# Moving the pair sums of the second key chunk to GpSimd and reordering the front units of the maxima in an attention block

## The chip, the cores and the metric

The kernel runs on one core of a Trainium2 chip, as one launch. The metric is the device time of that launch in microseconds (us). A core has five engines that each work through their own queue in order: TensorE (PE in the profile; PEld are its weight loads), VectorE (DVE), ScalarE (ACT), GpSimd (POOL) and SyncE (SP, which here issues nearly all DMAs). They wait for each other by semaphores. The stated times are 1812.58, 1813.54 and 1829.46 us; their median is 1813.54.

## The reference

One transformer block with adaptive layer norm, sequence 2048, width 512, 32 heads of 16, inner width 1792, all in float32:

```
mod = silu(c) @ w_mod                    # sa, ca, ga, sb, cb, gb
h = layernorm(x) * (1 + ca) + sa
q, k, v = h @ wqkv                       # 32 heads of width 16
o = softmax(q k^T / 4) v                 # full, 2048 x 2048 per head
x = x + ga * (o @ wo)
h = layernorm(x) * (1 + cb) + sb
out = x + gb * (gelu(h @ w1 + b1) @ w2 + b2)
```

## The kernel before, in words

Every matmul operand is split into a rounded high part and a low part, and a product is made of three matmuls (`mm3`, line 290): high by high, low by high, high by low.

**Units.** The heads are taken in 8 groups of 4, the queries in 4 blocks of 512. A unit `u` is one group and one block of queries; group `u // 4` gives its keys. For each unit the kernel first needs the largest score of every query and head, and then, in a second pass, the exponentials and their product with the values. The maxima of the first nine units (0 to 8, `NU1 = 9`) are made early, between the matmuls of the projections. Those of the other units are made within the attention, nine units ahead of the exponentials.

**Pair maxima.** The early maxima use a trick that halves the reductions: the maximum of a and b is (a + b)/2 + |a - b|/2. For groups 0 to 3 (key chunks `k` = 0 and 1) the kernel therefore stores, besides the keys, sums and differences of the keys of two neighbouring blocks of 512 (`kpm_d`). They are made in `proj_qk`: for an even block `b` the key projection is copied from PSUM to `k2` (line 308); for the odd block VectorE makes sum and difference from PSUM and `k2` (line 313), ScalarE rounds them to the high part (line 314), GpSimd makes the low part (line 320), and two DMAs store them (line 322). Each result is read by a front unit as `kpm[u // 4]`, loaded by `build_k` (line 350). In `pair_slot` a slot "V" multiplies queries by the differences (line 417) and ScalarE takes the absolute value (line 424); a slot "U", two places later, multiplies by the sums, and VectorE's custom instruction adds and reduces (line 428). Each slot has two matmuls of 48 rows that use different rows of the array. When the last slot of a unit is done, `max_rows` finishes its maxima with two small GpSimd operations, a transpose on VectorE (line 445), and four small stores (line 448).

**The stage.** After a first loop over the four blocks come 34 items in a fixed order. Items 0 to 9 are the last ten tiles of the values (tiles 6 to 15 of 16; `proj_v`, line 333 copies a tile from PSUM to one of the `vst` buffers, line 335 stores it). Items 10 to 17 are the projections with chunk k = 1, items 18 to 25 with k = 2, items 26 to 33 with k = 3; within a chunk the blocks b = 0 to 3 follow each other, keys (w = 1) ahead of queries (w = 0). Between the matmuls of an item stand "visits": from item 6 on five visits of two slots each, six in items 7, 14, 21 and 28. Unit number v in the order begins with visit 16 v and needs 16 slots of each kind; 144 visits fill the stage exactly. PSUM has two banks (`sc`) for the projections here and six (`mx`) for the slots. A projection's evacuation is line 303 on ScalarE (high part), line 304 on VectorE (low part), and what is left of it (`rest`: stores and GpSimd work) is issued with the first visit of the next item. Functions that a unit leaves over (`todo`) are run one at the end of each item.

**Loads.** At item 12 the keys of group 0 for the attention are loaded into `kq[0]`, then the values of group 0 (`load_v(0)`), then the weights of chunk 3. At item 21 the pair sums of group 2 go into the tile `kts[0]`, which units 0 to 3 have used; unit 8 needs them. At item 32 the keys of group 2 go into `kts[1]`, which units 4 to 7 have used; unit 9, the first maximum inside the attention, needs them. After the stage the keys of group 1 go into `kts[0]`.

**The weights of a chunk** are split in `split_w`: ScalarE rounds (line 172), GpSimd subtracts (line 174), at item 12 for chunk 2 and at item 20 for chunk 3.

Of the kernel before, what the change touches and what calls it, by code (L numbers as in the profile page):

```python
# [31 lines left out]
KR = 3 * DH  # L32
KX = KR + 2
NM = 32
NU1 = 9
FILL0 = 6
VISIT = 2
OP0 = 1
# [12 lines left out]
def block_kernel(ctx: ExitStack, tc: tile.TileContext, x, wqkv, wo, w1, b1, w2, b2, c, w_mod, out):  # L51
# [59 lines left out]
    b2_b = const.tile([P, D], F32, name="b2_b")  # L111
    b1_c = const.tile([P, NF], F32, name="b1_c")

    lcm, lend = pool("lend")
# [7 lines left out]
    wslots = [wpool.tile([P, KC, D], FR, name=f"w{i}") for i in range(2)]  # L122
    vwcm, vwpool = pool("vwpool", side="right")
    vslots = [vwpool.tile([P, KC, D], FR, name=f"wv{i}") for i in range(2)]
    vst = [vwpool.tile([P, NG, VG], F32, name=f"vst{i}") for i in range(5)]
    acm, apool = pool("apool", side="right")
    c_c = apool.tile([P, KC], F32, name="c_c")
    s_c = apool.tile([P, KC], F32, name="s_c")
# [35 lines left out]
    def split_w(k):  # L164
        raw = raws.pop(k)
        if k < 4:
            t = wslots[k % 2].rearrange("p a (b n) -> p (a b) n", n=P).rearrange("p (h w k) n -> p h w k n", h=2, w=2)
            for w in (1, 0):
                if k == 0:
                    ve.tensor_copy(t[:, 0, w], raw[:, w])  # L170
                else:
                    ac.activation(t[:, 0, w], raw[:, w], AF.Copy)
                eng = ve if k == 0 and w else gp
                eng.tensor_tensor(t[:, 1, w], raw[:, w], t[:, 0, w].bitcast(F32), op=ALU.subtract)
# [122 lines left out]
    def proj_qk(b, k, w, fill=()):  # L297
        hi, lo = hT[b]
        ps = bank()
        mm3(ps, [w_hi[k][:, w, i] for i in range(KC)], [w_lo[k][:, w, i] for i in range(KC)],  # L300
            [hi[:, i] for i in range(KC)], [lo[:, i] for i in range(KC)], fill)
        parts = tpool.tile([P, 2, TB], FR, tag="parts", name="parts", bufs=4)
        ac.activation(parts[:, 0], ps, AF.Copy)
        ve.tensor_tensor(parts[:, 1], ps, parts[:, 0].bitcast(F32), op=ALU.subtract)
        pair = w and k < 2
        if pair and b % 2 == 0:
            k2[k] = tpool.tile([P, TB], F32, tag="k2", name="k2", bufs=1)
            ac.activation(k2[k], ps, AF.Copy)
        if pair and b % 2:
            pm = [tpool.tile([P, TB], F32, tag="pm", name="pm", bufs=2) for _ in range(2)]  # L310
            pmh = [tpool.tile([P, 2, TB], FR, tag="parts", name="pmh", bufs=4) for _ in range(2)]
            for i, op in enumerate((ALU.add, ALU.subtract)):
                ve.tensor_tensor(pm[i], ps, k2[k], op=op)
                ac.activation(pmh[i][:, 0], pm[i], AF.Copy)

        def rest():
            st[0].dma_start(qk_d[w][k][:, :, b * TB : (b + 1) * TB].rearrange("a p t -> p a t"), parts.bitcast(F32))
            if pair and b % 2:
                for i in range(2):
                    gp.tensor_tensor(pmh[i][:, 1], pm[i], pmh[i][:, 0].bitcast(F32), op=ALU.subtract)  # L320
                    t0 = (b - 1 + i) * TB
                    st[0].dma_start(kpm_d[k][:, :, t0 : t0 + TB].rearrange("a p t -> p a t"), pmh[i].bitcast(F32))

        return rest

# [79 lines left out]
    def pair_slot(kind, n):  # L405


        u, i = divmod(n, 16)
        if u not in left:
            mxs[u] = small.tile([P, 2, 2, 4, 2], F32, tag="mxf", name="mxf")  # L410
            left[u] = 16
        p, qc, r = i // 8, (i // 2) % 4, i % 2
        t0 = (2 * r + (kind == "V")) * TB
        pss = [bank_mx() for _ in range(2)]
        for a, ps in enumerate(pss):
            rows = slice(a * 64, a * 64 + KR)
            te.matmul(ps, qmx[u][rows, p, qc * P : (qc + 1) * P], kpm[u // NB][rows, p, t0 : t0 + TB],  # L417
                      start=True, stop=True)
        if kind == "V" and i == 2:
            load_qm(u + 1)  # L420
        if kind == "V":
            for a, ps in enumerate(pss):
                vabs[n, a] = tpool.tile([P, TB], F32, tag="cp", name="cp", bufs=6)
                ac.activation(vabs[n, a], ps, AF.Abs)  # L424
            return []
        for a, ps in enumerate(pss):
            v = vabs.pop((n, a))
            ve.tensor_tensor_reduce(v, ps, v, -0.5, 3.0e38, ALU.add, ALU.min, mxs[u][:, p, a, qc, r : r + 1])  # L428
        left[u] -= 1
        return [] if left[u] else [max_rows(u)]  # L430
# [134 lines left out]
    for n, (k, b, w) in enumerate(items):  # L565
        if n == 1:
            close(acm)
            st[0] = sy
        if n == 8:
            build_k(kts[1], kpm_d[0], 1)  # L570
            for t in kts:
                one_rows(t)
        if n == nv + 1:
            close(vwcm)
            kqcm, kqpool = pool("kqpool")
            kq = [kqpool.tile([P, 2, S], FR, name="kq0")]
            one_rows(kq[0])
            vgcm, vgpool = pool("vgpool", bufs=2)
            qcm, qpool = pool("qpool")
        if n == nv + 2:  # L580
            load_k(0, kq[0])
            load_v(0)
        if n == nv + 11:
            kpm[2] = kts[0]
            build_k(kts[0], kpm_d[1], 2)
        if n == nv + 22:
            load_k(2, kts[1])
        if n == nv + 18:
# [37 lines left out]
    x2a = [epool.tile([P, 4, D], F32, name=f"x2a{i}") for i in range(2)]  # L626
    o_b = epool.tile([P, 4, D], F32, name="o_b")
    xn_b = epool.tile([P, 4, D], F32, name="xn_b")

# [360 lines left out]
```

## Time and profile before

| what | value |
|---|---|
| median of the runs | 1813.54 us (1812.58 to 1829.46) |
| the profiled execution | 1810.16 us, span of its instructions 1808.4 us |
| busy: PE, DVE, ACT, POOL | 1782.5, 1421.2, 1362.0, 251.7 us |
| mean granted TensorE clock | 0.977 |
| HBM | 105.85 MB read, 35.86 MB written |

A row of the profile's timeline gives the start, the length, the engine, the line of the kernel, the operation with its tiles (out<-in) and shape, and in brackets how long the engine was idle ahead of it and what ended that. A row of the windows gives a stretch of time, the busy time of each engine in it, the granted clock of TensorE (1.00 is full speed), and the use of the DMA engines. Matmuls are pipelined, so that a busy TensorE is not one at its peak. The stage of the 34 items runs from about 76 us to 332 us in the profiled execution, the attention from there to about 1400 us, and the second half of the block to the end.

### The profile page before, as it was taken

How to read it: one execution, taken by the hardware profiler on the slowest of the kernel's cores; microseconds unless marked ns; L12 is line 12 of the kernel's file. 1: busy time of each engine (PE TensorE's matmuls, PEld its weight loads, DVE VectorE, ACT ScalarE, POOL GpSimd, SP SyncE). 2: the span in 40 equal slices, each digit the busy share in tenths (PEclk: the TensorE clock that was granted, in tenths of full speed). 3: DMA queues.
4: the chain of work that ended last, by engine and by line, in shares of the span. 5: the costliest groups of instructions: out<-in, count | busy, mean ns of one | idle time of the engine just before them, and what ended most of it. 6: DMA issues, size and time to landing. Idle time of an engine off the chain costs nothing.

```text
span 1808.4 us, 29238 instructions
## 1 busy us (share of the span) xinstructions
PE 1782.5 (99%) x10554; PEld 912.8 (50%) x10554; DVE 1421.2 (79%) x2595; ACT 1362.0 (75%) x2590; POOL 251.7 (14%) x273
## 2 busy tenths in 40 slices
PE   8999999999999999999999999999999999999998
PEld 6754455434433333434334333343333477788887
DVE  6377799889888888888888888888887377738453
ACT  3476688799999999999999999999998732222222
POOL 3301000001000000000000000000002044545562
PEclk9996699999999999999999999999998999999999
DMA  7867253931311311321321101101112054423341
GB/s 272 246 134 162 79 123 107 141 66 46 58 37 34 55 40 35 49 46 34 50 45 34 38 23 30 42 22 27 30 54 94 30 174 135 128 72 109 107 121 47
DMA packets 123808, 143.64 MB, mean 79 GB/s; under 512 B 38896, under 2 KB 72688, under 8 KB 121712
## 3 DMA queue, kind: packets, MB, share of 16 engines
q1 hardware_dynamic: 120352, 135.02, 30.3%
q10 hardware_dynamic: 3312, 6.76, 1.0%
q8 instruction: 83, 1.36, 0.3%
q14 instruction: 61, 0.50, 0.1%
HBM read 105.85 MB, written 35.86 MB: 78 GB/s over the span
## 4 chain that ended last, share of the span: by engine, by line
PE 91%; DVE 3%; DMA 2%; issue 2%; POOL 1%; SPq 1%; ACT 1%; DVEq 0%; POOLq 0%; ACTq 0%
PE pv L657 28%; PE mx L400 19%; PE sc L290 15%; PE sc L824 13%; PE mx L417 6%; PE mx L888 5%; PE pv L888 2%; PE sc L764 1%; DMA kt<-qk 1%; PE mx L764 1%; DVE glo L871 0%; POOL w2l L695 0%; DMA wmod<-in_w_mod_dram 0%; DMA rb<-rden 0%; PE sc L252 0%
## 5 line engine op out<-in xcount | busy, mean ns | idle before, releaser
L825 ACT ACTIVATE p<-sc 128x512 f32<-128x512 f32 x2048 | 1055.1, 615 | 52.2 <-PE sc L824 26.1
L402 DVE TENSOR_REDUCE mxs<-mx 128x1 f32<-128x512 f32 x1472 | 927.9, 684 | 120.1 <-PE sc L824 83.6
L657 PE MATMUL pv<-p,vg 128*32 128x512 f32 x4096 | 549.4, 608 | 0.0
L824 PE MATMUL sc<-qst,kq 50*128 50x512 f32 x1024 | 286.5, 439 | 1.6 <-DVE mxf L428 1.6
L824 PE MATMUL sc<-qst,kt 50*128 50x512 f32 x1024 | 282.3, 431 | 0.0
L400 PE MATMUL mx<-kq,qmx 48*128 48x512 f32 x768 | 264.5, 431 | 3.7 <-DVE mxs L402 3.4
L400 PE MATMUL mx<-kt,qmx 48*128 48x512 f32 x704 | 240.9, 429 | 2.3 <-DMA kt<-qk 2.3
L400 PEld LDWEIGHTS mx<-kq,qmx 48*128 48x128 f32 x768 | 123.8, 185 | 235.6 <-DVE mxs L402 214.3
L428 DVE CUSTOM_DVE_ANT_0 cp<-mx,cp 128x512 f32<-128x512 f32 x288 | 185.4, 687 | 50.8 <-PE mx L417 45.0
L400 PEld LDWEIGHTS mx<-kt,qmx 48*128 48x128 f32 x704 | 113.8, 185 | 211.8 <-DVE mxs L402 191.6
L867 ACT ACTIVATE g<-sc,b_c 128x512 f32<-128x512 f32 x56 | 38.6, 690 | 238.8 <-PE sc L290 238.8
L424 ACT ACTIVATE cp<-mx 128x512 f32<-128x512 f32 x288 | 157.5, 598 | 56.7 <-PE mx L417 54.8
L657 PEld LDWEIGHTS pv<-p,vg 128*32 128x32 f32 x4096 | 81.2, 108 | 181.5 <-issue 170.1
L441 POOL CAST m<-mn 128x16 fp32r<-128x16 f32 x32 | 6.3, 197 | 1149.0 <-DVE mn L435 1149.0
L824 PEld LDWEIGHTS sc<-qst,kq 50*128 50x128 f32 x1024 | 127.1, 187 | 33.0 <-ACT p L825 22.9
L871 DVE TENSOR_TENSOR glo<-g,ghi 128x512 fp32r<-128x512 f32 x56 | 58.6, 1047 | 96.2 <-ACT ghi L870 96.2
L824 PEld LDWEIGHTS sc<-qst,kt 50*128 50x128 f32 x1024 | 125.6, 185 | 10.0 <-ACT p L825 3.1
L417 PE MATMUL mx<-kt,qmx 48*128 48x512 f32 x576 | 126.4, 495 | 3.6 <-DVE mxf L428 2.9
L693 POOL TENSOR_TENSOR w1l<-w1r,w1h 128x512 fp32r<-128x512 f32 x56 | 76.8, 1372 | 154.0 <-DVE w1h L692 133.9
L290 PE MATMUL sc<-hThi,w 128*128 128x512 f32 x256 | 93.2, 474 | 3.3 <-DVE hThi L258 3.3
L417 PEld LDWEIGHTS mx<-kt,qmx 48*128 48x128 f32 x576 | 61.5, 202 | 69.2 <-DVE mxf L428 27.3
L695 POOL TENSOR_TENSOR w2l<-w2r,w2h 128x512 fp32r<-128x512 f32 x56 | 81.1, 1448 | 6.6 <-DVE w2h L694 6.2
(145 smaller groups left out, 1644.3 us busy)
## 6 DMA issues: line engine op xcount, KB each, us to landing
w1r<-in_B_w_dram SPq DMA_DIRECT2D x56, 256.0 KB
w2r<-in_B_w_dram SPq DMA_DIRECT2D x56, 256.0 KB
qk<-parts SPq DMA_DIRECT2D x25, 512.0 KB
qmx<-qk SPq DMA_DIRECT2D x192, 64.0 KB
qst<-qk SPq DMA_DIRECT2D x192, 64.0 KB
wmod<-in_w_mod_dram SPq DMA_DIRECT2D x6, 1024.0 KB
kq<-qk SPq DMA_DIRECT2D x24, 256.0 KB
kt<-qk SPq DMA_DIRECT2D x24, 256.0 KB
```

The costliest lines, as they stand in the source:

```text
L290: te.matmul(ps, p, q, start=i == 0, stop=i == len(terms) - 1)
L400: te.matmul(ps, qmx[u][rows, p, qc * P : (qc + 1) * P], kst[u // NB][rows, p, kr * TB : (kr + 1) * TB], start=True, stop=True)
L402: ve.tensor_reduce(mxs[u][:, p, a, qc, kr : kr + 1], ps, axis=AX.X, op=ALU.max, negate=True)
L417: te.matmul(ps, qmx[u][rows, p, qc * P : (qc + 1) * P], kpm[u // NB][rows, p, t0 : t0 + TB], start=True, stop=True)
L424: ac.activation(vabs[n, a], ps, AF.Abs)
L428: ve.tensor_tensor_reduce(v, ps, v, -0.5, 3.0e38, ALU.add, ALU.min, mxs[u][:, p, a, qc, r : r + 1])
L657: te.matmul(cur_pv[0][32 * j : 32 * (j + 1)], vg[g][:, kc, j * VW : j * VW + 32], pt.pop((s, j)), start=kc == 0, stop=kc == NKC - 1)
L693: gp.tensor_tensor(alo, a, ahi.bitcast(F32), op=ALU.subtract)
L695: gp.tensor_tensor(blo, b, bhi.bitcast(F32), op=ALU.subtract)
L824: te.matmul(ps, k[r0 : r0 + KX, p, kc * P : (kc + 1) * P], q[r0 : r0 + KX, p], start=True, stop=True)
L825: ac.activation(pb, ps, AF.Exp, scale=SCALE)
L888: te.matmul(acc[qb][t], p[:, sl], q, start=f == 0 and n == 0, stop=f == NF - 1 and n == 2)
```

## The change

- In `proj_qk` for chunk k = 1 both blocks of a pair are copied from PSUM by ScalarE (`k2[0]`, `k2[1]`). GpSimd makes sum, difference and their high and low parts from the two copies; the difference overwrites `k2[0]`. The two stores are put into `todo` behind an empty entry and so go out two items after the one in which GpSimd's work is issued. For k = 0 the engines stay as they are, and the difference is made in place.
- The buffers: `parts` five instead of four, `pm` one instead of two, `k2` two tiles instead of one, `vst` four instead of five; `b2_b` moves to a pool that is opened later.
- For chunks 2 and 3 GpSimd rounds the weights in `split_w`, not ScalarE.
- The front units run in the order 0 to 5, 8, 6, 7. Unit 8 now begins with visit 96, which is in item 24, and units 6 and 7 follow; `kts[1]` is used to the end of the stage and `kts[0]` up to item 27.
- The loads: the pair sums of group 2 at item 20 (was 21), the values of group 0 at item 25 (was 12), the keys of group 2 at item 29 into `kts[0]` (was 32, into `kts[1]`), the keys of group 1 after the stage into `kts[1]` (was `kts[0]`).

```diff
+FRONT = (0, 1, 2, 3, 4, 5, 8, 6, 7, 9)
+NU1 = len(FRONT) - 1
...
-    vst = [vwpool.tile([P, NG, VG], F32, name=f"vst{i}") for i in range(5)]
+    vst = [vwpool.tile([P, NG, VG], F32, name=f"vst{i}") for i in range(4)]
...
+                elif k > 1:
+                    gp.tensor_copy(t[:, 0, w], raw[:, w])
...
-        parts = tpool.tile([P, 2, TB], FR, tag="parts", name="parts", bufs=4)
+        parts = tpool.tile([P, 2, TB], FR, tag="parts", name="parts", bufs=5)
...
-        if pair and b % 2 == 0:
-            k2[k] = tpool.tile([P, TB], F32, tag="k2", name="k2", bufs=1)
-            ac.activation(k2[k], ps, AF.Copy)
+        if pair and (k or b % 2 == 0):
+            k2[b % 2] = tpool.tile([P, TB], F32, tag=f"k2{b % 2}", name="k2", bufs=1)
+            ac.activation(k2[b % 2], ps, AF.Copy)
         if pair and b % 2:
-            pm = [tpool.tile([P, TB], F32, tag="pm", name="pm", bufs=2) for _ in range(2)]
-            pmh = [tpool.tile([P, 2, TB], FR, tag="parts", name="pmh", bufs=4) for _ in range(2)]
-            for i, op in enumerate((ALU.add, ALU.subtract)):
-                ve.tensor_tensor(pm[i], ps, k2[k], op=op)
-                ac.activation(pmh[i][:, 0], pm[i], AF.Copy)
+            pm = [tpool.tile([P, TB], F32, tag="pm", name="pm", bufs=1), k2[0]]
+            pmh = [tpool.tile([P, 2, TB], FR, tag="parts", name="pmh", bufs=5) for _ in range(2)]
+            if not k:
+                for i, op in enumerate((ALU.add, ALU.subtract)):
+                    ve.tensor_tensor(pm[i], ps, k2[0], op=op)
+                    ac.activation(pmh[i][:, 0], pm[i], AF.Copy)
+
+        def pair_store():
+            for i in range(2):
+                t0 = (b - 1 + i) * TB
+                st[0].dma_start(kpm_d[k][:, :, t0 : t0 + TB]..., pmh[i].bitcast(F32))
 
         def rest():
             st[0].dma_start(qk_d[w][k][:, :, b * TB : (b + 1) * TB]..., parts.bitcast(F32))
             if pair and b % 2:
-                for i in range(2):
+                for i, op in enumerate((ALU.add, ALU.subtract)):
+                    if k:
+                        gp.tensor_tensor(pm[i], k2[1], k2[0], op=op)
+                        gp.tensor_copy(pmh[i][:, 0], pm[i])
                     gp.tensor_tensor(pmh[i][:, 1], pm[i], pmh[i][:, 0].bitcast(F32), op=ALU.subtract)
-                    t0 = (b - 1 + i) * TB
-                    st[0].dma_start(kpm_d[k][:, :, t0 : t0 + TB]..., pmh[i].bitcast(F32))
+                if k:
+                    new.extend([lambda: None, pair_store])
+                else:
+                    pair_store()
...
-        u, i = divmod(n, 16)
+        v, i = divmod(n, 16)
+        u = FRONT[v]
...
-            load_qm(u + 1)
+            load_qm(FRONT[v + 1])
...
             load_k(0, kq[0])
-            load_v(0)
-        if n == nv + 11:
+        if n == nv + 10:
             kpm[2] = kts[0]
             build_k(kts[0], kpm_d[1], 2)
-        if n == nv + 22:
-            load_k(2, kts[1])
+        if n == nv + 15:
+            load_v(0)
+        if n == nv + 19:
+            load_k(2, kts[0])
...
-    load_k(1, kts[0])
+    load_k(1, kts[1])
```

In the last part `n` is the item and `nv` is 10.

More of the change, by code (lines that the diff above doesn't have):

```diff
@@ L34 @@
 NM = 32
-NU1 = 9
+FRONT = (0, 1, 2, 3, 4, 5, 8, 6, 7, 9)
+NU1 = len(FRONT) - 1
 FILL0 = 6
@@ L110, in block_kernel @@
     gb_b = const.tile([P, D], F32, name="gb_b")
-    b2_b = const.tile([P, D], F32, name="b2_b")
     b1_c = const.tile([P, NF], F32, name="b1_c")
@@ L305, in proj_qk @@
         pair = w and k < 2
-        if pair and b % 2 == 0:
-            k2[k] = tpool.tile([P, TB], F32, tag="k2", name="k2", bufs=1)
-            ac.activation(k2[k], ps, AF.Copy)
+        if pair and (k or b % 2 == 0):
+            k2[b % 2] = tpool.tile([P, TB], F32, tag=f"k2{b % 2}", name="k2", bufs=1)
+            ac.activation(k2[b % 2], ps, AF.Copy)
         if pair and b % 2:
-            pm = [tpool.tile([P, TB], F32, tag="pm", name="pm", bufs=2) for _ in range(2)]
-            pmh = [tpool.tile([P, 2, TB], FR, tag="parts", name="pmh", bufs=4) for _ in range(2)]
-            for i, op in enumerate((ALU.add, ALU.subtract)):
-                ve.tensor_tensor(pm[i], ps, k2[k], op=op)
-                ac.activation(pmh[i][:, 0], pm[i], AF.Copy)
+            pm = [tpool.tile([P, TB], F32, tag="pm", name="pm", bufs=1), k2[0]]
[7 more added lines that the diff above has]
+                t0 = (b - 1 + i) * TB
+                st[0].dma_start(kpm_d[k][:, :, t0 : t0 + TB].rearrange("a p t -> p a t"), pmh[i].bitcast(F32))
         def rest():
@@ L318, in rest @@
             if pair and b % 2:
-                for i in range(2):
+                for i, op in enumerate((ALU.add, ALU.subtract)):
+                    if k:
+                        gp.tensor_tensor(pm[i], k2[1], k2[0], op=op)
+                        gp.tensor_copy(pmh[i][:, 0], pm[i])
                     gp.tensor_tensor(pmh[i][:, 1], pm[i], pmh[i][:, 0].bitcast(F32), op=ALU.subtract)
-                    t0 = (b - 1 + i) * TB
-                    st[0].dma_start(kpm_d[k][:, :, t0 : t0 + TB].rearrange("a p t -> p a t"), pmh[i].bitcast(F32))
+                if k:
+                    new.extend([lambda: None, pair_store])
+                else:
+                    pair_store()
         return rest
@@ L626, in block_kernel @@
     x2a = [epool.tile([P, 4, D], F32, name=f"x2a{i}") for i in range(2)]
+    b2_b = epool.tile([P, D], F32, name="b2_b")
     o_b = epool.tile([P, 4, D], F32, name="o_b")
```

## The prediction

> **What bounds the kernel now.** First the page: its span, the busy times and the line of the granted clock.
>
> ```profile
> span 1808.4 us, 29238 instructions
> ...
> PE 1782.5 (99%) x10554; PEld 912.8 (50%) x10554; DVE 1421.2 (79%) x2595; ACT 1362.0 (75%) x2590; POOL 251.7 (14%) x273
> ...
> PEclk9996699999999999999999999999998999999999
> ```
>
> TensorE is busy nearly throughout, so time can be won only where it does the same work more slowly. The clock line names the place: slices 3 and 4 (each 45.2 us) stand at 0.6. All but one of the edits lie in or at the edge of that stage, items 0 to 33, in which TensorE alternates projections with the maxima of the front units. Its progress is the number of reductions on line 428 (two records each, with the read of the accumulator). The windows of that line alone count them:
>
> ```profile
> 131.00:249.00 118.00, 80.17 (x249) 0.77 0.54 123
> 249.00:331.80 82.80, 72.72 (x227) 1.00 0.40 99
> 153.14:180.44 27.30, 15.33 (x47) 0.50 0.56 171
> 194.10:221.40 27.30, 14.85 (x46) 0.50 0.32 112
> ```
>
> The columns are length, VectorE busy (records), granted clock, DMA share, GB/s. The second row is the stage undisturbed: 227 records in 82.8 us, 0.365 us each. At that pace the 249 records of the first row need 90.8 us and took 118.0: **27.2 us are lost.** Two stretches of exactly 27.3 us ran at half clock; their 47 and 46 records need 17.1 and 16.8 us, so they lost 10.2 and 10.5, together 20.7. The other 6.5 are stops.
>
> What starts a stretch? The timeline at its head, at the evacuation of items 12 and 16 (both k = 1, w = 1, b odd):
>
> ```profile
> 148.63 1.28 DVE L313 TENSOR_TENSOR pm<-sc,k 128x512 f32<-128x512 f32 x2
> ...
> 149.40 1.22 ACT L314 ACTIVATE pmh<-pm 128x512 fp32r<-128x512 f32 x2 [1.42 <-DVE pm L313]
> ...
> 150.11 2.52 POOL L320 TENSOR_TENSOR pmh<-pm,pmh 128x512 fp32r<-128x512 f32 x2 [6.16 <-ACT pmh L314]
> ...
> 150.57 1.10 PE L417 MATMUL mx<-kt,qmx 48*128 48x512 f32 x2 [1.31 <-DVE mxf L428]
> ...
> 193.97 1.29 PE L417 MATMUL mx<-kt,qmx 48*128 48x512 f32 x2 [1.40 <-DVE mxf L428]
> ```
>
> The two sums stand in front of the reductions on VectorE and make ScalarE wait, the six maximum banks fill, and TensorE stops for 1.31 and 1.40 us. The windows of 3.41 us around such stops (after the length: PE, PEld, DVE, ACT, POOL busy, then clock, DMA share, GB/s):
>
> ```profile
> 9.78:13.19 3.41, 2.53 (x20) 1.47 (x20) 2.35 (x4) 0.00 (x0) 0.70 (x14) 1.00 1.11 363
> ...
> 146.31:149.72 3.41, 2.95 (x15) 1.27 (x11) 3.21 (x9) 1.89 (x4) 0.00 (x0) 1.00 0.96 111
> 149.72:153.14 3.42, 2.46 (x9) 1.15 (x9) 2.70 (x9) 2.97 (x7) 2.52 (x2) 1.00 1.21 150
> ...
> 190.68:194.10 3.42, 2.02 (x10) 0.91 (x9) 3.42 (x11) 2.02 (x5) 0.69 (x1) 1.00 0.00 0
> ...
> 334.04:340.87 6.83, 4.80 (x19) 2.22 (x19) 3.23 (x7) 3.97 (x8) 0.00 (x0) 0.50 1.07 283
> 1801.78:1805.19 3.41, 1.74 (x8) 1.12 (x6) 3.34 (x6) 0.00 (x0) 0.00 (x0) 1.00 0.50 186
> 1805.19:1808.40 3.21, 0.00 (x0) 0.00 (x0) 0.19 (x1) 0.00 (x0) 0.00 (x0) 1.00 0.35 130
> ```
>
> The third and fourth windows, with 9 and 10 matmuls, many of them of 48 rows as at 150.57, are followed by half clock. The second, with 0.46 us idle, is not. Busy time alone does not decide: the window from 1801.78 has only 1.74 us busy, and the next is still at 1.00. Its matmuls fill the array:
>
> ```profile
> 1803.13 0.39 PE L888 MATMUL pv<-w2h,glo 128*128 128x512 f32 x1
> ```
>
> So I take it that the array's work within such a window decides, which is a reading of these few windows and no more.
>
> **The change, part by part.**
>
> *The sums of items 12 and 16.* Gone from VectorE are two operations of 0.64 us (148.63), from ScalarE two casts of 0.61 (149.40); added on ScalarE is one copy out of the bank. So these items become like item 10, which already makes such a copy and no sums:
>
> ```profile
> 131.06 0.60 ACT L303 ACTIVATE parts<-sc 128x512 fp32r<-128x512 f32 x1
> ...
> 132.43 0.60 ACT L308 ACTIVATE k<-sc 128x512 f32<-128x512 f32 x1 [0.76 <-DVE parts L304]
> ...
> 133.15 0.92 PE L417 MATMUL mx<-kt,qmx 48*128 48x512 f32 x2 [0.21 <-DVE mxf L428]
> ...
> 139.15 0.60 ACT L303 ACTIVATE parts<-sc 128x512 fp32r<-128x512 f32 x1
> ...
> 317.05 0.60 ACT L303 ACTIVATE parts<-sc 128x512 fp32r<-128x512 f32 x1
> ...
> 324.45 0.60 ACT L303 ACTIVATE parts<-sc 128x512 fp32r<-128x512 f32 x1
> ```
>
> The copy waits for VectorE's subtraction on the same bank (0.76 us); TensorE then stops for 0.21 us, the clock stays, and evacuation to evacuation is 8.09 us instead of 7.40: 0.69 us. After the change four items pay that (10, 12, 14, 16): 2.8 us remain of the 6.5, so 3.7 of stops and 20.7 of half clock go: **-24.4.** Bounds: 0 (the clock falls anyway and the copies cost what the sums did) and -27.2.
>
> *GpSimd's added work.* Per pair, six operations of 128x512 where there were two. The subtraction is 1.26 us (150.11). The trace has no copy of that size on GpSimd; it lies between almost nothing and a subtraction, and I take the subtraction: 7.6 us. They are issued in item 13 or 17, and who waits for them is ScalarE's next write of k2 at the end of item 14 (the second sum is made in place there), more than an item of 7.40 us later, and the store. Cover gone (over twice as slow), ScalarE's Abs casts would queue behind that write. The next maxima rows on GpSimd come in items 15 and 18. The cast of the weights moves there too:
>
> ```profile
> 139.62 1.16 ACT L172 ACTIVATE w<-wraw 128x512 fp32r<-128x512 f32 x2
> ...
> 140.34 2.52 POOL L174 TENSOR_TENSOR w<-wraw,w 128x512 fp32r<-128x512 f32 x2 [20.96 <-ACT w L172]
> 140.39 0.68 DVE L428 CUSTOM_DVE_ANT_0 cp<-mx,cp 128x512 f32<-128x512 f32 x1
> ...
> 141.00 0.69 DVE L428 CUSTOM_DVE_ANT_0 cp<-mx,cp 128x512 f32<-128x512 f32 x1
> ```
>
> GpSimd stood idle for 20.96 us ahead of it, and the parts are used six items later: nothing. That ScalarE loses 1.16 us twice is inside the 6.5. While GpSimd works, VectorE's reductions keep their 0.61 us pitch, so I add nothing for contention.
>
> *The store, two projections later.*
>
> ```profile
> 195.65 1.33 SPq L322 DMA_DIRECT2D kpm<-pmh  x2
> ...
> 229.44 3.38 SPq L350 DMA_DIRECT2D kt<-kpm  x6
> ```
>
> The second pair's store now goes out after item 19 and its loads (line 350) at item 20, which hold SP's queue until the store has landed; the stores of later parts wait behind them, and a fifth buffer covers that. Unit 8 needs these sums in item 24 rather than 30: four items, over 29 us, against 1.33 and 3.38 us of issue plus landing. The query loads of the units now behind unit 8 only change places. The values of group 0 (from item 12 to 25) leave the most loaded part of the queue and are needed after item 33. All nothing; if the sums came late, unit 8 would stop TensorE by the lateness and risk a stretch of half clock.
>
> *Four value buffers instead of five.* Here the change adds a wait:
>
> ```profile
> 88.18 6.34 SPq L335 DMA_DIRECT2D v<-vst  x6
> ...
> 89.95 0.60 ACT L333 ACTIVATE vst<-sc 128x512 f32<-128x512 f32 x1 [2.20 <-PE sc L290]
> ...
> 92.55 0.86 PE L290 MATMUL sc<-wv,hThi 128*128 128x512 f32 x3
> ...
> 93.58 0.60 ACT L333 ACTIVATE vst<-sc 128x512 f32<-128x512 f32 x1 [3.03 <-DMA v<-vst]
> ```
>
> Value tile 11 (item 5) waits until 93.58 for the store of tile 6, issued at 88.18. With four buffers it is tile 10 that reuses it: its copy moves from 89.95 to 93.58 and ends at 94.18. Item 6 needs that bank of two, so TensorE starts it at about 94.2 instead of 92.55: 1.65 us, behind it item 6's first maxima. ScalarE was already held up by the same wait before, so part returns; I take **+1.1**, between 0 and +1.65.
>
> *Front of the attention.*
>
> ```profile
> 320.35 2.75 SPq L350 DMA_DIRECT2D kt<-qk  x6
> ...
> 330.72 0.97 PE L290 MATMUL sc<-hTlo,w 128*128 128x512 f32 x3
> ...
> 333.28 0.50 PE L824 MATMUL sc<-qst,kq 50*128 50x512 f32 x2 [1.60 <-DVE mxf L428]
> ...
> 336.07 0.76 PE L400 MATMUL mx<-kt,qmx 48*128 48x512 f32 x1 [2.29 <-DMA kt<-qk]
> ```
>
> Unit 9's keys, issued in item 32, arrive 2.29 us late. Unit 8's early turn frees their tile three items sooner (item 29, some 22 us), so this stop goes. The 1.60 us before it, VectorE's last reductions, stays. The half clock from 334.04 to 340.87 held 4.80 us of matmuls; if it stays whole, 2 us more of work falls into it and costs 1.0; if it goes, 2.4 come on top. **-2.3**, between -1.3 and -4.7. Where b2 lies changes no row.
>
> **Sum:** -24.4 + 1.1 - 2.3 = **-25.6 us**. The profiled execution took 1810.16 (span 1808.4, 1.8 around it) and becomes 1784.6; the median of the runs is 3.4 higher, so I forecast **1788**.
>
> A rule that speaks against this: the Trainium skill, "TensorE: Matmul & The Clock Gate" (part 1, and its section on oscillation), lets the clock fall after an idle window of about 3.4 us and return after one busy window of that length. The trace disagrees on both: stops of 1.31 and 1.40 us were enough, and two returns took 27.3 us.
>
> **Rivals.**
>
> 1. *The value wait costs a stretch of half clock.* Its 1.65 us are as long as the stops that did. For: a stretch in this stage lost 10.2 and 10.5. Against: ahead of and behind the wait stand full 128-row matmuls, as in the window from 1801.78, which kept its clock. 1788 + 10.4 = **1798**. The same time comes out if one of the pair items keeps its stretch.
> 2. *The stretches need no such stop.* If only idle windows of the full 3.41 us halve the clock, the sums are not the cause and both stretches stay: 1788 + 20.7 = **1809**. That is what the skill's clock page would give. Against: both begin within 5 us of the sums, and there is none elsewhere in the stage.
> 3. *Slower: the threshold lies below 0.5 us idle in a window.* Then the 0.21 us stops of the pair copies suffice at items 12 and 16 and the value wait adds a third stretch: 1788 + 20.7 + 10.4 = **1819**. It decides where half a microsecond idle is enough; the window from 146.31 (0.46 idle) and that from 9.78 (0.88 idle) speak against it.
>
> **How the numbers follow.** Forecast 0.61, rival 1 0.27, rival 2 0.07, rival 3 0.05. The forecast's own range is 1783 to 1793 (the bounds of the value wait and of the attention's front, and a few us on the pair copies); with rival 1 it reaches from 1782 to 1803, and the remaining 0.12 is rivals 2 and 3 and surprises. One per cent, about what a measurement of this kernel can tell from no change, is 1795.4 or less on the fast side: the forecast alone is there, 0.62. Rivals 1 to 3 lie within one per cent: 0.33. For slower by over 1% (1831.7) more than three stretches would be needed: 0.05.
>
> **What would show it.** Right: no half clock between 100 and 310 us; line 313 gone from items 12 and 16; their neighbours 8.1 us apart; the copy of value tile 10 with about 3.6 us idle behind a DMA, and a stop of about 1.5 us ahead of item 6; no wait for a DMA at the first maximum of the attention; the stage's end near 308. Wrong: a stretch of 27.3 us behind item 5, 12 or 16; ScalarE waiting for GpSimd at items 14 or 16; TensorE waiting for a DMA at unit 8's first matmul.

## The result, and the profile after

The changed kernel takes 1794.2 us, median of 16 runs (1787.4 to 1819.24); the kernel before takes 1813.37 beside it, median of 16 (1805.79 to 1832.27). The ratio is **0.9888 [0.9854, 0.9923]**: 1.1% faster. Forecast were 1788 us, which is the lowest of the 16 runs and not their middle: ten lie within 8 us of the lowest, six above. The median lies 1.2 us outside the forecast's own range (1783 to 1793) and inside the one with rival 1 (1782 to 1803). The profiled execution took 1787.71 us (forecast 1784.6, before 1810.16). Ratios, here and below, leave out runs of a kernel more than 1.5% above its fastest, so lowest and median stand beside them.

From the page after:

```profile
span 1785.6 us, 29238 instructions
...
PE 1763.4 (99%) x10554; PEld 906.1 (51%) x10554; DVE 1418.2 (79%) x2591; ACT 1360.9 (76%) x2584; POOL 261.6 (15%) x280
...
PEclk9999999999999999999999999999998999999999
```

The two sixes in the clock line are gone. TensorE is 19.1 us less busy with the same 10554 instructions. VectorE has lost four operations and ScalarE six; GpSimd has gained seven, for 9.9 us more of work: eight for the sums and four for the weights, less five small memsets of the fifth value buffer.

How much of it is the stage? Windows of the reduction line alone, from the evacuation of item 10 to that of item 33, before (line 428) and after (line 443). The columns are length, VectorE busy (records), granted clock, DMA share, GB/s:

```profile
131.06:331.77 200.71, 152.80 (x473) 0.86 0.48 113
```

```profile
132.25:308.96 176.71, 151.87 (x473) 1.00 0.57 136
```

The same 473 records take 24.0 us less, at full clock throughout. The timeline after, at items 10 and 12, with GpSimd's sums behind item 12:

```profile
132.25 0.61 ACT L306 ACTIVATE parts<-sc 128x512 fp32r<-128x512 f32 x1
...
134.33 0.98 PE L432 MATMUL mx<-kt,qmx 48*128 48x512 f32 x2 [0.20 <-DVE mxf L443]
...
140.40 0.60 ACT L306 ACTIVATE parts<-sc 128x512 fp32r<-128x512 f32 x1
...
147.70 0.60 ACT L306 ACTIVATE parts<-sc 128x512 fp32r<-128x512 f32 x1
...
149.74 1.28 POOL L330 TENSOR_TENSOR pm<-k,k 128x512 f32<-128x512 f32 x1 [4.79 <-ACT k L311]
151.09 0.61 POOL L331 CAST pmh<-pm 128x512 fp32r<-128x512 f32 x1
...
155.08 1.30 POOL L332 TENSOR_TENSOR pmh<-k,pmh 128x512 fp32r<-128x512 f32 x1
155.78 0.60 ACT L306 ACTIVATE parts<-sc 128x512 fp32r<-128x512 f32 x1
```

Item 10, with a copy behind it, lasts 8.15 us from evacuation to evacuation, item 11 7.30, item 12, again with a copy, 8.08. The stop behind item 10's copy is 0.20 us; behind item 14's it is 0.47 (experiment 6), and that item's copy costs more: 8.65 us to the next evacuation. GpSimd's six operations run from 149.74 to 156.38, 6.6 us, and nobody waits for them: item 13 is evacuated at 155.78 in their midst.

The place where the change adds a wait, at value tiles 9 and 10:

```profile
86.46 0.61 ACT L347 ACTIVATE vst<-sc 128x512 f32<-128x512 f32 x1 [2.20 <-PE sc L293]
87.28 7.37 SPq L349 DMA_DIRECT2D v<-vst  x6
...
92.81 0.60 ACT L347 ACTIVATE vst<-sc 128x512 f32<-128x512 f32 x1 [5.75 <-DMA v<-vst]
93.47 0.96 PE L293 MATMUL sc<-wv,hThi 128*128 128x512 f32 x3 [1.44 <-ACT vst L347]
```

And the front of the attention:

```profile
308.96 0.60 ACT L306 ACTIVATE parts<-sc 128x512 fp32r<-128x512 f32 x1 [1.56 <-issue]
...
310.46 0.50 PE L841 MATMUL sc<-qst,kq 50*128 50x512 f32 x2 [1.59 <-DVE mxf L443]
311.28 0.79 PE L414 MATMUL mx<-kt,qmx 48*128 48x512 f32 x1 [0.32 <-DVE parts L307]
...
314.37 1.08 PE L674 MATMUL pv<-p,vg 128*32 128x512 f32 x4
```

The first maximum (line 414) no longer waits for a DMA. The wait for VectorE before it stays at 1.59. From the last evacuation to the first product are 5.41 us; before they were 7.36 (331.77 to 339.13).

**Where the 22.8 us of span come from**, instruction against instruction: up to the value tiles -0.7 (tile 9 is copied at 87.15 before, at 86.46 after); value wait +1.9 (the lead goes from +0.7 to -1.2 at item 10's evacuation); items 10 to 33 -24.0; front of the attention -1.95. That is 24.8 at the first product, and 2.0 are given back behind it.

Whether the first 0.7 is the change's isn't known. What is given back belongs to the execution, not to the change: at the end of the attention half clock lasts 10.2 us before and 17.1 us after, and in a second profiled execution of the changed kernel (experiment 8) 10.2 us again. From the first product to the end the three take 1469.3, 1471.2 and 1467.0 us.

**The spread.** The granted clock of each run tells what sets it. The lowest run has a mean clock of 0.993, the one of 1811.55 us 0.975, the highest 0.970. Between the profiled execution (1787.71 us, 0.992) and that of 1811.55 the clock lacks 0.008 and 0.025 of the span, which is 28.6 and 90.5 us at half clock: 62 us more. A microsecond at half clock loses 0.374 us in this stage (the prediction's 10.2 of 27.3), so these make 23.1 us; measured are 23.8. So stretches of half clock like those of the stage account for the difference. Where they lie, a mean clock doesn't tell; a second profile of the changed kernel (experiment 8) has one in the stage.

### The profile page after: what moved, and what is told of

It is laid out like the page before. It is cut to its first block, busy times and chain, and to the rows that moved or that the text cites. A ratio compares the mean times of both kernels' runs of the same rounds, so it can differ in the third digit from the quotient of the medians.

```text
span 1785.6 us, 29238 instructions
## 1 busy us (share of the span) xinstructions
PE 1763.4 (99%) x10554; PEld 906.1 (51%) x10554; DVE 1418.2 (79%) x2591; ACT 1360.9 (76%) x2584; POOL 261.6 (15%) x280
## 4 chain that ended last, share of the span: by engine, by line
PE 90%; DVE 4%; DMA 2%; issue 2%; POOL 1%; SPq 0%; ACT 0%; DVEq 0%; POOLq 0%; ACTq 0%
PE pv L674 28%; PE mx L414 19%; PE sc L293 14%; PE sc L841 13%; PE mx L432 6%; PE mx L905 5%; PE pv L905 2%; PE sc L781 1%; PE mx L781 1%; DMA v<-vst 1%; DVE glo L888 0%; DVE cp L443 0%; POOL w2l L712 0%; PE sc L255 0%; DMA rb<-rden 0%
## 5 line engine op out<-in xcount | busy, mean ns | idle before, releaser
L414 PE MATMUL mx<-kt,qmx 48*128 48x512 f32 x704 | 241.6, 430 | 0.3 <-DVE parts L307 0.3
L432 PE MATMUL mx<-kt,qmx 48*128 48x512 f32 x576 | 117.9, 457 | 1.0 <-ACT cp L439 0.5
L293 PE MATMUL sc<-hThi,w 128*128 128x512 f32 x256 | 83.0, 430 | 3.8 <-DVE hThi L261 3.8
```

Source lines behind the costliest of these rows:

```text
L293: te.matmul(ps, p, q, start=i == 0, stop=i == len(terms) - 1)
L414: te.matmul(ps, qmx[u][rows, p, qc * P : (qc + 1) * P], kst[u // NB][rows, p, kr * TB : (kr + 1) * TB], start=True, stop=True)
```

## The experiments

**1. Is it the sums?** Everything of the change stays but the place of the sums: they go back to VectorE and ScalarE.

```diff
-        if pair and (k or b % 2 == 0):
+        if pair and b % 2 == 0:
             k2[b % 2] = ...
-            if not k:
+            if True:
                 for i, op in enumerate((ALU.add, ALU.subtract)):
                     ve.tensor_tensor(pm[i], ps, k2[0], op=op)
...
-                    if k:
-                        gp.tensor_tensor(pm[i], k2[1], k2[0], op=op)
-                        gp.tensor_copy(pmh[i][:, 0], pm[i])
```

> The changed kernel, but the sums of chunk k = 1 are made by VectorE and rounded by ScalarE again, as before the change; the store stays two projections later, the order of the units, the loads and the buffers stay changed. Theory A (the stops behind the sums halve the clock): two stretches of 27.3 us at half clock come back right behind items 12 and 16, the profiled time is about 24 us above the changed kernel's (some 1809 us of span against 1785.6). Theory B (the stretches have nothing to do with the sums, the order of units or loads removed them): no half clock between 100 and 300 us, at most 4 us slower than the changed kernel.

Measured: 1824.17 us (10 runs, 1809.69 to 1857.5), ratio 1.0046 [1.0003, 1.0089]; span of the profiled execution 1807.9. The whole gain is gone, and a little more. The trace at items 12 and 16, first the stops, then the windows around them:

```profile
155.71 1.33 PE L429 MATMUL mx<-kt,qmx 48*128 48x512 f32 x2 [1.43 <-DVE mxf L440]
...
200.64 1.24 PE L429 MATMUL mx<-kt,qmx 48*128 48x512 f32 x2 [1.59 <-DVE mxf L440]
```

```profile
152.63:156.04 3.41, 1.98 (x9) 0.79 (x9) 3.32 (x8) 1.96 (x4) 0.97 (x1) 1.00 0.91 100
156.04:186.76 30.72, 30.71 (x79) 13.76 (x78) 18.36 (x57) 16.12 (x31) 1.95 (x4) 0.50 0.39 110
197.00:200.41 3.41, 2.05 (x10) 0.78 (x8) 3.31 (x9) 1.89 (x4) 0.53 (x1) 1.00 0.00 0
200.41:210.65 10.24, 10.01 (x24) 4.72 (x24) 6.12 (x21) 5.84 (x12) 1.99 (x2) 0.50 0.15 53
```

Both stretches are back at their places, one of 30.7 us and one of 10.2, where the trace before had 27.3 twice. So the sums start them, and what a stretch costs is not fixed.

**2. The sums alone.** The kernel before with the change's projection part (GpSimd's sums, late store, four value buffers, five parts), with the units and the attention's loads in the old order.

> The kernel before, with the sums of chunk k = 1 on GpSimd, their late store, and the buffers that go with it (four for the values); order of units, loads and the rounding of the weights stay as before. Theory A: no half clock between 100 and 300 us, span about 1787 to 1789 (the ScalarE casts of the weights stay, about 1 us, and so does the wait for the keys of unit 9 at the front of the attention, 2.3 us). Theory B: both stretches stay, span near 1808.

Measured: 1804.97 us (10 runs, 1787.85 to 1828.33), ratio 0.9925 [0.9882, 0.9968]. The lowest run (1786.1 us of span) is near where the theory put it; the median is not. The profiled execution, 1826.6 us of span, shows why: a stretch of 88.7 us, in front of any sum, behind ScalarE's rounding of the weights at item 11.

```profile
141.08 1.16 ACT L171 ACTIVATE w<-wraw 128x512 fp32r<-128x512 f32 x2
...
142.78 0.98 PE L427 MATMUL mx<-kt,qmx 48*128 48x512 f32 x2 [0.31 <-ACT cp L434]
```

```profile
140.64:144.05 3.41, 3.10 (x13) 1.46 (x13) 3.18 (x10) 3.41 (x8) 2.25 (x2) 1.00 1.02 123
144.05:232.75 88.70, 88.70 (x231) 40.21 (x229) 52.78 (x158) 44.14 (x83) 14.14 (x19) 0.50 0.41 106
```

The stop ahead of it is 0.31 us, and the window has 13 matmuls and 3.10 us busy. Taking 0.374 us for each of the 88.7 leaves 1793 us.

**3. Stops made on purpose.** In the changed kernel, behind items 18 and 26, which have no sums: one sum with its ScalarE pass (item 18), two (item 26), written to scratch that nobody reads.

```diff
+        if (k, b, w) in FAKE:        # {(2, 0, 1): 1, (3, 0, 1): 2}
+            for tag in ("pm", "k20")[: FAKE[k, b, w]]:
+                z = tpool.tile([P, TB], F32, tag=tag, name="z", bufs=1)
+                ve.tensor_tensor(z, ps, parts[:, 0].bitcast(F32), op=ALU.add)
+                ac.activation(z, z, AF.Copy)
```

> The changed kernel with useless work behind two evacuations in which it has no sums: one 128x512 sum on VectorE and one ScalarE cast at item 18, two of each at item 26; results go nowhere. Theory A: the double dose stops TensorE for 1.2 to 1.5 us and a stretch of half clock of 27.3 us follows item 26, about 10 us plus 2 us of stops; the single dose stops it for about 0.5 us and the clock stays. Span about 1797 to 1799. Theory B: stops of that length change no clock: about 2 us slower than the changed kernel, 1788.

Measured: 1807.24 us (10 runs, 1793.32 to 1834.47), ratio 0.9944 [0.9902, 0.9987]; span 1807.9. Stops first, then the windows:

```profile
199.31 1.04 PE L438 MATMUL mx<-kt,qmx 48*128 48x512 f32 x2 [0.71 <-DVE mxf L449]
...
262.73 1.03 PE L438 MATMUL mx<-kt,qmx 48*128 48x512 f32 x2 [1.22 <-DVE mxf L449]
```

```profile
200.47:203.88 3.41, 3.41 (x9) 1.48 (x8) 1.49 (x7) 1.87 (x4) 0.00 (x0) 0.50 0.80 296
261.91:265.32 3.41, 2.55 (x10) 1.22 (x10) 2.67 (x9) 2.97 (x7) 0.00 (x0) 1.00 0.81 241
265.32:309.70 44.38, 44.38 (x116) 20.02 (x115) 26.97 (x81) 22.38 (x42) 0.42 (x2) 0.50 0.47 92
```

Two sums at a place that had no stop make one of 1.22 us and 44.4 us of half clock. One sum makes 0.71 us and a single window of 3.4, where none was expected. That such work starts a stretch, at a place that had none, is shown; that the stop must be over a microsecond is refuted.

**4. The value wait.** Two ways to take it away. The first lets the values' stores go out by SyncE's queue until item 6 instead of item 1, the second gives the fifth value buffer back and takes one from the parts.

```diff
         (values_by_act)
+        if n == 6:
             st[0] = sy
         (five_value_buffers)
-    vst = [... for i in range(4)]
+    vst = [... for i in range(5)]
-        parts = tpool.tile(..., bufs=5)    # and pmh
+        parts = tpool.tile(..., bufs=4)
```

In the first diff the line `st[0] = sy` is moved from `n == 1`: until then stores are issued by the other queue.

> The changed kernel, with the stores of value tiles 6 to 11 issued by ScalarE instead of SyncE, so that they don't stand behind the loads of the pair sums. If the copy of tile 10 waits for the store of tile 6 because that store is issued late (88.18 us before), it now goes out about 8 us earlier, the wait of 5.75 us and TensorE's stop of 1.44 us ahead of item 6 go, and the span is 1.5 to 2 us shorter than the changed kernel's. If the DMA engines themselves are what is late there, the wait stays and the time is the same. The stop costs no half clock in the changed kernel's profile, so no more than 2 us are expected.

> The changed kernel with five value buffers again; to make room the parts and pair sums have four buffers instead of five. If the copy of tile 10 waits for the fourth buffer, ScalarE's idle 5.75 us and TensorE's stop of 1.44 us ahead of item 6 go: item 6 ends about 1.7 us earlier, and no stretch of half clock can begin there. The price may show at items 15 and 16, where parts take the buffers of the pair sums whose store is deferred: 0 if the store has landed by then. Lowest run 1785.7 if nothing waits there.

The first: 1810.42 us (10 runs, 1793.24 to 1825.54), ratio 0.9956 [0.9914, 0.9998]. The value copies don't wait any more, and TensorE waits for the loads of the pair sums instead:

```profile
90.86 6.10 SPq L364 DMA_DIRECT2D kt<-kpm  x6
...
93.63 0.60 ACT L347 ACTIVATE vst<-sc 128x512 f32<-128x512 f32 x1 [2.19 <-PE sc L293]
...
99.56 1.50 PE L432 MATMUL mx<-kt,qmx 48*128 48x512 f32 x2 [4.84 <-DMA kt<-kpm]
```

```profile
99.59:140.55 40.96, 40.96 (x104) 18.32 (x104) 20.61 (x63) 20.05 (x37) 0.00 (x0) 0.50 0.45 80
```

4.84 us and a stretch of 41 us for a wait of 1.44: moving the stores moved the wait. That the traffic itself is the limit there (a DMA share of 0.92 from 80 to 95 us in the changed kernel) is likely, but not shown.

The second: 1788.03 us (10 runs, 1782.77 to 1803.19), ratio 0.9878 [0.984, 0.9915]. Lowest and median are 4.6 and 6.2 us under the changed kernel's, though the ratios do not tell the two apart. The profiled execution was the slowest of the ten (span 1801.3): the parts now wait for their store at item 13, and 47.8 us of half clock follow. First the wait and TensorE's next maxima, then the windows:

```profile
156.91 0.60 ACT L306 ACTIVATE parts<-sc 128x512 fp32r<-128x512 f32 x1 [0.53 <-DMA qk<-parts]
...
157.53 1.51 PE L432 MATMUL mx<-kt,qmx 48*128 48x512 f32 x4
```

```profile
157.32:160.73 3.41, 3.39 (x13) 1.35 (x11) 3.18 (x11) 2.85 (x6) 0.00 (x0) 1.00 0.58 171
160.73:208.52 47.79, 47.79 (x124) 21.76 (x123) 28.58 (x87) 24.28 (x46) 6.72 (x8) 0.50 0.23 82
```

Here the trace shows nearly no idle time ahead of the stretch. But the four maxima at 157.53, of which four like them 2.8 us earlier took 0.73 us, took 1.51, and the window has 13 matmuls, as many as that ahead of the stretch in experiment 2. The ends of matmuls are modelled, so a stop can hide in such a group.

**5. The copies.** The bank is read by ScalarE's first part, VectorE's subtraction and then ScalarE's copy, which costs the item 0.8 us. The sum of the two parts gives the same key back to within their rounding, and GpSimd can form it:

```diff
-            ac.activation(k2[b % 2], ps, AF.Copy)
+            if not k:
+                ac.activation(k2[b % 2], ps, AF.Copy)
...
+            if pair and k:
+                gp.tensor_tensor(k2[b % 2], parts[:, 0].bitcast(F32), parts[:, 1].bitcast(F32), op=ALU.add)
```

> The changed kernel, but ScalarE makes no copy of the keys of chunk k = 1 out of PSUM: GpSimd adds their stored high and low parts, one operation of 1.26 us more for each of the four key projections (items 10, 12, 14, 16). Theory A': the copies' stops (0.69 us of pace each) are what is left of the 6.5 us, and a stop as short as 0.2 to 0.3 us starts a stretch of half clock in some executions. Then items 11, 13, 15 and 17 take 7.3 us like the others, the undisturbed time is 2.8 us under the changed kernel's 1787.4 (some 1784.6), and fewer runs lie more than 8 us above the lowest one. Theory C (stretches come by chance, whatever the stops): 2.8 us lower, with the same spread of the runs.

Measured: 1780.23, 1783.39, 1805.06 and 1808.32 us, ratio 0.9889 [0.9787, 0.9991]. The first is the lowest of all runs of any kernel; two are some 25 us slower. The profiled one (span 1806.3) is of these. In it the four items last 7.31 to 7.33 us, as they should, but the value wait has done what rival 1 said:

```profile
96.40 1.65 PE L293 MATMUL sc<-wv,hThi 128*128 128x512 f32 x3 [2.08 <-ACT vst L350]
```

```profile
96.42:151.03 54.61, 54.61 (x141) 24.75 (x141) 27.34 (x84) 27.44 (x51) 0.42 (x2) 0.50 0.42 89
151.03:308.00 156.97, 156.96 (x681) 83.98 (x680) 150.50 (x462) 128.16 (x235) 27.77 (x36) 1.00 0.56 130
```

**6. The weights' cast back on ScalarE.** The two lines `elif k > 1: gp.tensor_copy(...)` are removed.

> The changed kernel, with the weights of chunks 2 and 3 rounded by ScalarE again (items 12 and 20). In the kernel with the sums alone moved, a stretch of 88.7 us of half clock began in one execution right behind that rounding, at a stop of 0.31 us. Theory A': stops of 0.3 us come back ahead of items 13 and 21, about 0.9 and 0.4 us of pace, and stretches begin there in some executions: lowest run about 1.3 us above the changed kernel's, median some 5 us above. Theory C: lowest run 1.3 us above, and the same spread.

Measured: 1792.89 us (10 runs, 1783.9 to 1826.16), ratio 0.9908 [0.9867, 0.9949]: not the 5 us more that were expected, and no difference from the changed kernel that ten runs show. In the profiled execution (span 1824.4) the rounding at item 11, with its stop of 0.31 us, kept the clock; the copy at item 14 lost it, for 99 us:

```profile
169.36 0.99 PE L430 MATMUL mx<-kt,qmx 48*128 48x512 f32 x2 [0.46 <-ACT cp L437]
```

```profile
142.97:146.38 3.41, 3.10 (x13) 1.40 (x12) 2.74 (x10) 2.49 (x6) 2.75 (x4) 1.00 1.04 120
...
170.28:269.27 98.99, 98.99 (x257) 45.05 (x256) 58.70 (x177) 49.36 (x93) 10.08 (x14) 0.50 0.34 88
```

So a copy can start a stretch. It is not a copy that the change adds (those are of items 12 and 16): the kernel before copies item 14's keys too, inside its first stretch of half clock. In the changed kernel's trace the same stop kept the clock:

```profile
167.15 0.99 PE L432 MATMUL mx<-kt,qmx 48*128 48x512 f32 x2 [0.47 <-ACT cp L439]
```

What the rounding alone costs stays open.

**7. Group 2's keys at the old time** (`n == nv + 19` becomes `nv + 22`).

> The changed kernel, with the keys of group 2 loaded at item 32 again instead of 29. Theory: they arrive late again, TensorE's first maximum of the attention waits 2 to 2.5 us for a DMA, and the time from the last evacuation of the stage to the first step of the products is 2 to 3 us longer. Rival: it is the half clock there, 6.8 us in both profiles, that sets this time, and the same work falls into it either way: under 1 us of difference.

Measured: 1804.22 us (10 runs, 1787.17 to 1820.1), ratio 0.9938 [0.9889, 0.9987]. Its median is worth little beside that spread; the trace (span 1789.5) is worth more:

```profile
311.25 0.60 ACT L306 ACTIVATE parts<-sc 128x512 fp32r<-128x512 f32 x1 [1.54 <-issue]
...
315.00 0.74 PE L414 MATMUL mx<-kt,qmx 48*128 48x512 f32 x1 [1.73 <-DMA kt<-qk]
...
318.06 1.08 PE L674 MATMUL pv<-p,vg 128*32 128x512 f32 x4
```

The wait for the DMA is back, 1.73 us, and from the last evacuation to the first product are 6.81 us against 5.41. So the early load is worth 1.4 us here, between the two expectations (2 to 3 us, and under 1).

**8. All known stops of the stage gone.** Together: the keys from the parts (5), five value buffers and five parts. Room is made by scratch: the sums of item 8 use the tile "k21", those of items 12 and 16 a used weight buffer. The second kernel also swaps the order in which the attention's banks are laid, `open_psum(sc=4, mx=3, pv=1)`. Beside them ran the changed kernel again.

> The changed kernel with GpSimd making the keys of chunk k = 1 from their stored parts (no ScalarE copy) and five value buffers; room for the fifth value buffer comes from the sums' scratch tile, which now lies in a used weight buffer, so parts keep five buffers. Theory A': with both kinds of stops gone (4 x 0.69 us and 1.7 us) the undisturbed time is 4.5 us under the changed kernel's, some 1783, nothing between items 5 and 33 starts a stretch of half clock, and most runs lie within 5 us of the lowest; median 7 to 10 us under the changed kernel's. Theory C (stretches come by chance): 4.5 us lower, with the same spread.

> The kernel without those stops, and at the front of the attention the score banks are opened ahead of the maximum banks, so that the first exponentials' banks are old projection banks. If the stop of 1.6 us there is a wait for single banks, TensorE starts the scores up to 1.6 us earlier and the half clock of 6.8 us there may go: 2 to 4 us shorter. If the wait is for all banks of the old pools together, the stop stays and the time is the same.

> The changed kernel as it is, beside the two that follow on the same chip. Its time is 1787.4 where no stretch of half clock falls into the stage, and 10 us more for each 27 us of half clock; ratio to the kernel before 0.985 to 0.992.

| kernel | runs | lowest | median | highest | ratio to before |
|---|---|---|---|---|---|
| changed, again | 12 | 1788.07 | 1795.24 | 1812.05 | 0.9905 [0.9864, 0.9945] |
| no stops | 6 | 1781.69 | 1783.99 | 1785.32 | 0.9828 [0.9779, 0.9877] |
| no stops, other banks | 6 | 1780.29 | 1782.87 | 1783.46 | 0.9820 [0.9776, 0.9864] |

All twelve runs without the stops are below the lowest of the 28 of the changed kernel, and each kernel's six lie within 3.7 us. The changed kernel's own profiled execution in this comparison (span 1788.5) has a stretch of 13.7 us, right behind the copy of item 14:

```profile
168.92 0.98 PE L432 MATMUL mx<-kt,qmx 48*128 48x512 f32 x2 [0.48 <-ACT cp L439]
```

```profile
171.20:184.90 13.70, 13.70 (x38) 6.15 (x34) 8.02 (x24) 7.00 (x13) 0.26 (x2) 0.50 0.40 140
```

The trace of "no stops", from the value tiles to the end of the stage:

```profile
90.00:100.00 10.00, 10.00 (x43) 6.09 (x42) 2.01 (x7) 5.01 (x10) 0.00 (x0) 1.00 1.01 272
100.00:308.00 208.00, 206.48 (x890) 109.74 (x890) 198.42 (x609) 168.48 (x309) 28.56 (x40) 1.00 0.58 133
308.50:315.30 6.80, 6.48 (x27) 3.30 (x26) 4.20 (x8) 4.70 (x10) 0.25 (x2) 0.50 0.89 180
```

TensorE does not stop once from 90 to 100, where the value wait was. From there to the end of the stage the clock is full; half clock follows at the attention's front. There the other bank order didn't do what it was for:

```profile
307.06 1.22 PE L849 MATMUL sc<-qst,kq 50*128 50x512 f32 x3 [2.43 <-DVE parts L307]
```

The stop became 2.43 us (1.62 in "no stops"), for another operation of VectorE, and half clock follows it, 10.2 us instead of 6.8. The two kernels' times agree within their spread, so what that stop is worth stays unsettled.

## Why the prediction was right, and where it was not

**The sums, -24.4: measured -24.0.** The mechanism holds both ways: with the sums back the stretches are back, with sums put elsewhere stretches come up there. Items 10, 12 and 16 last 8.15, 8.08 and 8.07 us, where 8.09 was read from item 10 before. Item 14, which the prediction took to be like them, lasts 8.65: against the 7.30 of an item without a copy the four lose 3.8 us, not 2.8. So -24.0 is closer to -24.4 than its parts are; what made up for it was not worked out.

**GpSimd, the store and the loads, nothing: nothing.** From item 6 to the end of the stage TensorE waits for no DMA, and ScalarE never for GpSimd. The bound taken from the subtraction was too high, since a cast is 0.61 us against 1.28; it didn't matter.

**The value buffers, +1.1, at most +1.65: measured +1.9**, above the bound. The stop ahead of item 6 is 1.44 us (expected about 1.5). The copy comes at 92.81, 3.55 us later than the pace of the value tiles (2.80) would have it, and 3.6 were forecast; its 5.75 us of idle time hold also the 2.20 that ScalarE waits ahead of every such copy.

**The attention's front, -2.3: measured -1.95 there.** Of it, the early load holds 1.4 (experiment 7). The half clock there stayed whole, from 311.24 to 318.07 us, as assumed.

**The step that failed** is "TensorE then stops for 0.21 us, the clock stays", and with it the listing of forecast and rival 1 as alternatives of which one happens. The 0.21 us were read from item 10 alone; behind item 14's copy the stop is 0.47 us. And the same stop does both, execution by execution: item 14's cost nothing in the changed kernel's first trace, 13.7 us of half clock in its second and 99 us in experiment 6; the value wait cost 1.9 us in one trace and 54.6 us of half clock in experiment 5. So the forecast's time is that of the runs with no stretch (lowest 1787.4), and the median, 6 us above, is a mixture of it with rival 1 and worse. Part of that agreement is luck: for an execution without a stretch 1784.6 was forecast and 1787.7 measured, and the 3.4 us that were added for the spread of the kernel before fill that gap. The prediction had the sign to doubt this in its own quotes: it called the reading of a few windows no more than that, and then let it decide. Its price of 10.4 us a stretch was as fixed as it should not have been: stretches of the stage, in all the traces, last 3.4, 10.2, 13.7, 27.3, 27.3, 30.7, 41.0, 44.4, 47.8, 54.6, 88.7 and 99.0 us, all a whole number of windows of 3.41 us; at 0.374 us lost for each microsecond, an estimate from the trace before, that is 1 to 37 us. Nor do the chances add up: rivals 1 to 3 make 0.39, where 0.33 is given for within one per cent, and the 0.12 beside forecast and rival 1 is rivals 2 and 3 alone, with nothing left for surprises.

**Rivals 2 and 3.** Rival 2, that the sums are not the cause, fell with experiments 1 and 3, and with it the rule of the Trainium skill ("TensorE: Matmul & The Clock Gate", part 1) that it takes an idle window of about 3.4 us to lose the clock and one busy window to win it back: stops of 0.31 to 2.08 us were enough, and TensorE was busy for all of 99.0 us at half clock. The same page of the Trainium skill has another section, on a second failure mode, by which short idle times between groups of matmuls that cycle through PSUM make the clock swing; with that the traces agree (0.71 us of idle, 3.4 us of half clock). Rival 3, that half a microsecond is enough, is half right: sometimes it is. Its sign was wrong, for the stretches it predicts came in some runs and not in all.

**What decides, as far as the traces show it.** All changes of the clock in a trace lie on one grid of 3.41 us. Count what the array does in each window of that grid: a matmul of 128 rows as 1, one of 48 rows as 48/128, with the part of it that lies in the window, each 0.43 us long at half clock (the distance of two 128-row matmuls there) and half of that at full clock. All thirteen traces together, from 76 to 306.5 us, give this:

- Of the windows at full clock, the 13 that half clock follows hold 6.14 at most, the other 708 hold 6.22 or more.
- Of the windows at half clock, the eleven that end a stretch hold 5.96 to 6.14; of the other 131 only three hold more than 5.87.

One border near 6.1 orders both, which fits the prediction's reading: the array's work within a window decides, not idle time alone. The stage as a rule does 8.9 in a window at full clock and 5.3 at half, which is below the border; so a stretch keeps itself up, though TensorE is busy, until a window happens to hold more 128-row matmuls. And the stop behind item 14's copy leaves 6.63 and 6.26 where the clock stayed (the changed kernel's first trace, experiment 7) but 6.14 and 6.08 where it fell (its second trace, experiment 6), because the grid lies differently in each execution: a window starts 0.1 us ahead of that item's evacuation in the first trace and 1.4 us behind it in the second. The kernels without stops have 7.3 or more in every window from 85 to 300 us. This is a count made afterwards: the ends of matmuls are modelled, the margin is thin, with a weight of a quarter or a half for 48 rows the groups overlap, and no run was made to test it.

**What stays open:** whether that border holds for other matmuls than these, and what the rounding of the weights alone costs. A window with 13 matmuls and 3.10 us busy lost the clock in experiment 2. In experiment 6 the window from 142.97 around the same rounding, again 13 matmuls and 3.10 us, kept it; by the count they hold 5.7 and 6.7.

## What to carry to other kernels

Where TensorE alternates matmuls of many rows with ones of few and another engine's queue stands between it and its next bank, stops far under a microsecond are worth removing, not for their own length but for the half clock that they can start; twelve runs without them were faster and agreed within a few microseconds. A wide spread between runs of one kernel can be a symptom of such stops, as here: compare lowest, median and each run's granted clock before believing one trace. Where a queue is loaded, as with the value stores, a different order moved the wait to another engine; a buffer more took it away.

## What the runs showed of the hardware

- In the stage half clock came in whole windows of 3.41 us, 1 to 29 of them, with TensorE busy nearly from end to end. It came behind windows with little work of the array (at most 6.14 by the count above) and ended with ones of 5.96 or more.
- An f32 to f32r cast of 128x512 on GpSimd took 0.61 us, half of a subtraction of that size (1.28).
- Three reads of one PSUM bank by ScalarE, VectorE and ScalarE again ran one after the other: the copy waited 0.76 us for the subtraction, and an item lost 0.8 us by it (8.08 against 7.30), nearly all of which came back when GpSimd summed the parts in SBUF instead (7.31).
